# Hash attention and a PReLU MLP in fp32 on one core: the division first in VectorE's round, with weight steps behind its reciprocal, and w_out's operand sums in the MLP's first blocks

## The chip, the cores and the metric

One core of a Trainium2 chip. The metric is the device time of one execution in microseconds (us).

## The reference

```python
# B, H, S, D = 4, 8, 768, 64; proj is 64 x 6; w_in 512 x 2048, w_out 2048 x 512
q_bits, k_bits = (q @ proj > 0), (k @ proj > 0)          # six sign bits per row
mask = bucket(q_bits)[..., :, None] == bucket(k_bits)[..., None, :]
scores = where(mask, q @ k.T / sqrt(D), -1e9)
attn = softmax(scores) @ v
x = attn.transpose(0, 2, 1, 3).reshape(3072, 512)
h = x @ w_in
out = (max(h, 0) + alpha * min(h, 0)) @ w_out
```

All in fp32. Both products of the MLP are made by a seven-product scheme on 2 x 2 blocks (7 products of half size instead of 8), so weights and activations need sums of their blocks as operands.

## The kernel before

Attention runs in 32 rounds, two for each pair of heads. TensorE makes scores of round u+1, then `av` and the row sums `sm` of round u. VectorE adds up probabilities (accp, accd), divides (st, rc, rr, dn, x), and beside that prepares the MLP's weights: each of 32 pieces (16 of w_in, 16 of w_out) is split in two parts in six steps, and four operand sums per group of pieces are made. The finished groups are stored to DRAM (w_in_s, w_out_s) and loaded again in the MLP (`wi` for each first-stage block, `wl` for each second-stage product).

```python
def divide(u, between=lambda: None):
    ...                                                  # cut: tiles
    do(DVE.transpose(a, sums[u]))                        # st
    do(DVE.tensor_scalar(r, a..., S * EPS, None, op0=ALU.add))      # rc
    do(DVE.reciprocal(rr, r...))                         # rr
    for q0 in (0, D):                                    # four small copies on GpSimd
        q1 = q0 + 32
        do(POOL.tensor_copy(rr[q0 : q0 + 32, 1], rr[q1 : q1 + 32, 1]))
        do(POOL.tensor_copy(rr[q1 : q1 + 32, 0], rr[q0 : q0 + 32, 0]))
    between()                                            # here: one or two operand sums
    do(DVE.transpose(d, rr...))                          # dn
    do(DVE.scalar_tensor_tensor(x, av[u], vsum[pi], d, ...))        # x, frees av's bank

for u in range(UNITS):                                   # cut to the parts concerned
    scores(u, 1)
    if u < last:
        scores(u + 1, 0)
    if u:
        divide(u - 1, lambda: weight_sums(1 if u < HW else 2))
    add_last(u)                                          # accd
    add_total(u)
    if u < last:
        add_first(u + 1)                                 # accp; its second half by an accumulating DMA
    ...                                                  # cut: hash bits, q and k turns
    if u < last:
        weight_parts(u + 1)                              # four of the six steps
    attend(u)                                            # av
    totals(u)                                            # sm
    if u < last:
        weight_sum(u + 1)                                # the last two steps
        weight_group(u + 1)                              # queues four sums and the store
    ...
    load_weight(u + 4)
    ...                                                  # at odd u: loads of v, q, k of later pairs

for j, (b, what, n) in enumerate(blocks):                # MLP, cut
    ...
    if what == "1":
        load_w(b * NI + n + 2)                           # wi, double-buffered
        if n >= NI - 2:
            load_w2(b, n - NI + 2)                       # wl
```

In the traces, f_0 to f_7 are the eight blocks of the MLP's first stage and z_1 to z_7 the products of its second; pt are the probabilities, qn, kn and vn the loaded pieces of q, k and v, and vd is a small TensorE step of a range check that needs the largest values (top) from VectorE.

`do` keeps an instruction at its place in its engine's program; transfers issued without it are placed by a scheduler that may move them ahead. Nearly all transfers go through the one queue of SyncE (SPq in the traces; 127.18 of 141.64 MB).

Of the kernel before, what the change touches and what calls it, by code (L numbers as in the profile page):

```python
# [8 lines left out]
F32 = mybir.dt.float32  # L9
# [3 lines left out]
ALU = mybir.AluOpType  # L13
# [393 lines left out]
def fast_path(  # L407
# [60 lines left out]
    NI = NF // 2  # L468
    NM = 7
    w_in_s = dram.tile([NI, P, NM, 2, P], F32, name="w_in_s")  # L470
    w_out_s = dram.tile([NM, P, NI, DM // 2], F32, name="w_out_s")
    x_s = dram.tile([B, NP, P, S], F32, name="x_s")
    NW = NK * NF // 2
    wmax = const.tile([P, NW], F32, name="wmax")
# [68 lines left out]
    def piece(i):  # L543
# [8 lines left out]
        o = n + NI * m  # L552
        return moe_w_out[o * P : (o + 1) * P]

    def load_weight(i):
        if i < NW:
            raw[i] = pool.tile([P, 512], moe_w_in.dtype, name=f"raw{i}", tag="raw", bufs=3)
            nc.sync.dma_start(raw[i], piece(i))

# [5 lines left out]


    def weight_abs(i):
        lo, hi = halves(i)
        wx[i] = pool.tile([P, 512], F32, name=f"wx{i}", tag="wx")
        do(ACT.activation(wx[i], hi.bitcast(F32), AF.Abs))  # L570

    def weight_parts(i):
        lo, hi = halves(i)
        x = wx[i]
        wr[i] = r = pool.tile([P, 512], F32, name=f"wr{i}", tag="wr", bufs=1)
        do(DVE.tensor_scalar(x, x, HI_MIN, None, op0=ALU.max, op1=ALU.max, accum_out=wmax[:, i : i + 1]))  # L576
        do(DVE.tensor_scalar(
            x.bitcast(U32), x.bitcast(U32), 3, 0xC0000000, op0=ALU.logical_shift_left, op1=ALU.bitwise_xor,
        ))
        do(DVE.tensor_scalar(r.bitcast(U32), x.bitcast(U32), 0x7F800000, None, op0=ALU.bitwise_and))  # L580
        do(DVE.scalar_tensor_tensor(r, lo, 2.0 ** -52, r, op0=ALU.mult, op1=ALU.mult))

    def weight_sum(i):


        lo, hi = halves(i)
        x, r = wx[i], wr[i]
        if i < HW:
            n, m = divmod(i, 4)
            if m == 0:  # L590
                wst[n] = pool.tile([P, NM, 4, P], F32, name=f"wsi{n}", tag="wsi")
            slot = (0, 5, 1, 2)[m]
            dst = wst[n][:, slot].rearrange("p i f -> p (i f)")
        else:
            n, m = divmod(i - HW, 2)
            if m == 0:
                wst[HW + n] = pool.tile([P, NM, DM // 2], F32, name=f"wso{n}", tag="wso")
            w = wst[HW + n]
            dst = w[:, 0:6:5] if m == 0 else w[:, 1:3]
        turned = i < HW and m == 3  # L600
        do(DVE.scalar_tensor_tensor(
            r, x, -1.0 if turned else 1.0, r, op0=ALU.mult, op1=ALU.subtract if turned else ALU.add,
        ))
        if i >= HW:
            hi, r = (t.rearrange("p (a f) -> p a f", a=2) for t in (hi, r))
        do(DVE.scalar_tensor_tensor(
            dst.bitcast(U32), hi, 0x80000000, r.bitcast(U32), op0=ALU.bitwise_and, op1=ALU.bitwise_xor,
        ))
# [2 lines left out]

    def weight_group(i):

        if i < HW and i % 4 == 3:
            n = i // 4
            w = wst[n]
        elif i >= HW and i % 2 == 1:
            n = (i - HW) // 2
            w = wst[HW + n]
        else:  # L620
            return
        s1 = ALU.subtract if i < HW else ALU.add
        sums4 = ((3, 5, s1, 2), (5, 0, ALU.subtract, 5), (4, 3, ALU.subtract, 0), (6, 1, ALU.subtract, 4))

        def one(to, a, op, c):
            do(DVE.tensor_tensor(w[:, to], w[:, a], w[:, c], op=op))

        def store():
            if i < HW:
                c, kk = divmod(n, 2)  # L630
                for ii in range(4):
                    nc.sync.dma_start(w_in_s[4 * c + ii][:, :, kk], w[:, :, ii])
            else:
                nc.sync.dma_start(w_out_s[:, :, n].rearrange("m p d -> p m d"), w)

        for x in sums4:
            sums_due.append((one, x))
        sums_due.append((store, ()))

    def weight_sums(count):  # L640
# [266 lines left out]
    def load_w2(b, n):  # L907

        if n < 7:
            t = late[0].tile([P, NI, 2 * H2], F32, name=f"wl{b}_{n}", tag="wl")  # L910
            nc.sync.dma_start(t, w_out_s[SIDES[ORDER[n]][0]])
            for m, kh, dh in ((0, 0, 0), (1, 1, 0), (2, 1, 1), (21, 0, 1)):
                w2[b, n, m] = t.rearrange("p n (f i) -> p n i f", i=2)[:, kh * HK : (kh + 1) * HK, dh]

    def sides_g(b, n):
        t = g_m[b, SIDES[ORDER[n]][1]]
# [138 lines left out]
    weight_abs(0)  # L1055
    weight_parts(0)
    weight_sum(0)
    load_weight(3)
    for name in "qk":
        turn(1, name)  # L1060
    weight_abs(1)
    for u in range(UNITS):
        pi, g = divmod(u, NCH)
        scores(u, 1)
        if u < last:
            scores(u + 1, 0)
        if u:
            divide(u - 1, lambda: weight_sums(1 if u < HW else 2))
        add_last(u)
        add_total(u)  # L1070
        if u < last:
            add_first(u + 1)
        else:
            now = ff1(0, 0)
            now.step(1)
            now.step(5)
        if g == 0 and pi + 1 < NPAIR:
            hash_bits(pi + 1)
        if g == 1 and pi + 2 < NPAIR:
            turn(pi + 2, "q")  # L1080
            turn(pi + 2, "k")
        if u < last:
            weight_parts(u + 1)
        else:
            weight_sums(4)
        attend(u)
        totals(u)
        if u < last:
            weight_sum(u + 1)
            weight_group(u + 1)  # L1090
        else:
            divide(u)
        if g == 1 and pi + 2 < NPAIR:
            load(pi + 2, "v")
        load_weight(u + 4)
        if u == HW + 2:
            load_w(0)
            load_w(1)
            load_x(0)
        if HW + 4 <= u < HW + 8:  # L1100
            sum_x(0, u - HW - 4, DVE)
        if u + 2 < NW:
            weight_abs(u + 2)
        if u == 1:
            setup_alpha()
        if g == 1:
            for name in "qk":
                magnitude(pi, name)
                if pi + 3 < NPAIR:
                    load(pi + 3, name)  # L1110
# [2 lines left out]
    late = []  # L1113
    attn.close()
    late.append(ctx.enter_context(tc.tile_pool(name="late", bufs=2)))
    blocks = [(b, what, n) for b in range(B) for what, count in (("1", NI), ("2", 7)) for n in range(count)]


    for j, (b, what, n) in enumerate(blocks):
# [24 lines left out]
            sum_g2(b, n2, 5)  # L1144
        if j == 4:
            verdict()
        if what == "1":
            load_w(b * NI + n + 2)
            if n >= NI - 2:
                load_w2(b, n - NI + 2)  # L1150
        else:
            load_w2(b, n + 2)
            if b + 1 < B:
                if n == 0:
                    load_x(b + 1)
                if n == 6:
                    for m in range(4):
                        sum_x(b + 1, m, DVE)
# [41 lines left out]
```

## Time and profile before

| | before |
|---|---|
| time, median (lowest to highest) of 4 runs, in the rounds of the changed kernel | 918.46 us (917.09 to 919.78) |
| span of the profiled run | 916.6 us |
| start of the last `sm` (end of attention) | 363.73 us |
| start of the MLP's second stage (first z_1a) | 433.47 us, so 69.74 us after the last sm |
| from z_1a to the end | 483.1 us |
| TensorE waits for VectorE's x in attention | 14.2 us, 18 times |

The last `sm` and the first z_1a cut the span in three: attention, the MLP's first stage, the rest. The profile's lines of attention stand in the prediction. The prediction also reads the time from issue to landing of the wi loads in the MLP's first stage (the view of the tile wi, window 345 to 432 us).

```profile
DMA to landing us min/median/max: 4.3/4.6/6.5
```

Its longest, 6.5 us, was the load that flew just behind two 1 MB loads.

### The profile page before, as it was taken

What the parts mean: (1) busy time and instruction counts of PE and PEld (TensorE: products, weight loads), DVE (VectorE), ACT (ScalarE), POOL (GpSimd) and SP (SyncE); (2) the same over time, 40 slices, a digit from 0 to 9 for tenths busy, and PEclk for the clock granted to TensorE, in tenths of its full rate; (3) what the DMA queues carried; (4) which work ended last, traced back from release to release, by engine and by line L of the source; (5) the groups of instructions that cost most, each with busy time, mean ns of one, the idle gap of its engine ahead of it and who ended that gap; (6) DMA issues with size and microseconds to landing.
All of it is one profiled execution on the core that took longest, in us unless ns stands there. A gap on an engine that the chain in (4) does not pass through costs nothing.

```text
span 916.6 us, 15648 instructions
## 1 busy us (share of the span) xinstructions
PE 888.8 (97%) x5885; PEld 591.8 (65%) x5885; DVE 758.0 (83%) x1353; ACT 409.9 (45%) x735; POOL 70.2 (8%) x178
## 2 busy tenths in 40 slices
PE   8999999999999999999999999999999999999996
PEld 4444444444444444556999556998556998556996
DVE  4888888899999998677989667989777989768985
ACT  7888887788877874222111222111222112222111
POOL 1122121221111121000000000000000000000000
PEclk9999999999999999999999999999999999999998
DMA  9677979799877754534433534333535343521242
GB/s 236 147 182 189 240 196 283 183 219 248 215 187 190 205 133 121 192 112 143 143 115 110 160 121 148 134 109 115 159 118 160 122 124 102 180 95 40 93 152 59
DMA packets 132677, 141.64 MB, mean 155 GB/s; under 512 B 78048, under 2 KB 120816, under 8 KB 129008
## 3 DMA queue, kind: packets, MB, share of 16 engines
q1 hardware_dynamic: 121872, 127.18, 45.3%
q0 software_dynamic: 8704, 12.58, 8.5%
q8 instruction: 48, 0.79, 0.4%
q10 hardware_dynamic: 2016, 0.79, 0.3%
q14 instruction: 37, 0.30, 0.1%
HBM read 100.67 MB, written 27.26 MB: 140 GB/s over the span
## 4 chain that ended last, share of the span: by engine, by line
PE 58%; DMA 1%; DVE 1%; POOL 0%; ACT 0%; issue 0%; ACTq 0%; DVEq 0%; POOLq 0%
PE z_4a L838 2%; PE f_2a L838 2%; PE z_3a L838 2%; PE z_6a L838 2%; PE z_2a L838 2%; PE z_1a L838 2%; PE z_5a L838 2%; PE f_5a L838 2%; PE f_7a L838 2%; PE f_6a L838 2%; PE f_4a L838 2%; PE f_3a L838 2%; PE f_0a L838 2%; PE z_7a L838 2%; PE f_1a L838 2%; PE z_2c L838 1%
## 5 line engine op out<-in xcount | busy, mean ns | idle before, releaser
L723 ACT ACTIVATE pt<-sc 128x768 f32<-128x768 f32 x192 | 152.6, 813 | 63.9 <-PE sc L718 61.9
L718 PE MATMUL sc<-qT,kT 64*128 64x384 f32 x768 | 155.3, 483 | 0.0
L751 PE MATMUL av<-pt,vn 128*32 128x384 f32 (+1 forms) x1536 | 130.6, 488 | 14.4 <-DVE x L792 14.2
L751 PEld LDWEIGHTS av<-pt,vn 128*32 128x32 f32 x1536 | 46.8, 110 | 91.0 <-issue 62.8
L718 PEld LDWEIGHTS sc<-qT,kT 64*128 64x128 f32 x768 | 68.3, 188 | 34.8 <-issue 34.6
L888 DVE TENSOR_TENSOR g<-g,g 128x384 f32<-128x384 f32 x128 | 68.3, 554 | 2.2
L718 PE MATMUL sc<-qb,kb 64*128 64x384 bf16 x384 | 63.5, 324 | 2.8 <-ACT kb L706 1.0
L936 DVE TENSOR_TENSOR gs<-g,gs 128x768 f32<-128x768 f32 x56 | 53.3, 952 | 1.0
L928 DVE TENSOR_TENSOR ws<-wl 128x512 f32<-128x512 f32 x56 | 38.5, 687 | 18.8 <-DMA wl<-w_out_s 18.7
L936 DVE TENSOR_TENSOR gs<-g 128x768 f32<-128x768 f32 x56 | 53.2, 951 | 0.0
L733 POOL DMA_DIRECT2D accp<-pt x32 | 38.5, 1204 | 191.2 <-issue 75.2
L884 DVE SCALAR_TENSOR_TENSOR g<-h,alpha 128x384 f32<-128x384 f32 x32 | 19.7, 617 | 33.4 <-ACT h L877 33.4
L718 PEld LDWEIGHTS <-kb 64*128 64x128 bf16 x384 | 19.5, 94 | 34.4 <-issue 12.3
L695 ACT ACTIVATE qb<-hs,hb 32x384 bf16<-32x384 f32 x62 | 35.5, 573 | 1.1
L789 DVE STREAM_TRANSPOSE dn<-rr 128x384 f32<-128x384 f32 x32 | 18.5, 578 | 21.1 <-POOL rr L787 21.1
L741 DVE TENSOR_TENSOR accd<-accd,accp 128x768 f32<-128x768 f32 x32 | 30.7, 958 | 5.2 <-DMA accp<-pt 4.2
L738 DVE TENSOR_TENSOR accd<-accd,pt 128x768 f32<-128x768 f32 x32 | 30.7, 959 | 3.3
L732 DVE TENSOR_TENSOR accp<-pt,pt 128x768 f32<-128x768 f32 x32 | 30.4, 951 | 2.6 <-ACT pt L723 2.6
L737 DVE TENSOR_TENSOR accd<-pt,pt 128x768 f32<-128x768 f32 x32 | 30.4, 949 | 0.0
L948 DVE TENSOR_TENSOR m<-m,m 128x768 f32<-128x768 f32 (+1 forms) x40 | 28.3, 709 | 1.0 <-ACT m L954 0.3
L706 ACT ACTIVATE kb<-hs,hb 64x384 bf16<-64x384 f32 (+1 forms) x47 | 27.1, 577 | 0.6
L576 DVE TENSOR_SCALAR_CACHE_REDUCE wx<-wx 128x512 f32<-128x512 f32 x32 | 21.7, 679 | 2.9 <-ACT wx L570 2.9
(334 smaller groups left out, 1782.6 us busy)
## 6 DMA issues: line engine op xcount, KB each, us to landing
wi<-w_in_s SPq DMA_DIRECT2D x32, 896.0 KB, 4.6
wl<-w_out_s SPq DMA_DIRECT2D x28, 1024.0 KB, 4.9
accp<-pt POOLq DMA_DIRECT2D x32, 384.0 KB, 4.4
raw<-in_moe_w_in_dram SPq DMA_DIRECT2D x16, 512.0 KB, 4.6
raw<-in_moe_w_out_dram SPq DMA_DIRECT2D x16, 512.0 KB, 3.7
w_in_s<-wsi SPq DMA_DIRECT2D x16, 448.0 KB, 5.9
w_out_s<-wso SPq DMA_DIRECT2D x8, 896.0 KB, 4.5
vn<-in_v_dram SPq DMA_DIRECT2D x16, 384.0 KB, 5.2
```

Of the source, the lines that this page charges most:

```text
L695: do(ACT.activation(bits["q", pi][D * s : D * s + 32, cols], ps["q"][c : c + 32, half, :CW], AF.Sign, bias=hb[c : c + 32],))
L718: do(PE.matmul(sc[:, s, :CW], what["k", pi][r, ks], what["q", pi][r, qs], start=first, stop=not first,))
L723: do(ACT.activation(pt[:, :, :CW], sc[:, :, :CW], AF.Exp, scale=SCALE / DOWN))
L732: do(DVE.tensor_tensor(accp[u], p(u, 0), p(u, 1), op=ALU.add))
L733: nc.gpsimd.dma_start(accp[u], p(u, 2), accum_op=ALU.add)
L738: do(DVE.tensor_tensor(accd[u], accd[u], p(u, 5), op=ALU.add))
L741: do(DVE.tensor_tensor(accd[u], accd[u], accp[u], op=ALU.add))
L751: do(PE.matmul(av[u][D * s + t : D * s + t + 32, :w], nat["v", pi][:, s, kc * D + t : kc * D + t + 32], prob[u, kc][:, s, :w], start=(kc = ...
L838: do(PE.matmul(self.ps[bank], self.left(left, k), self.right(right, k), start=start and k == 0, stop=k == self.nk - 1, skip_group_check=no ...
L888: do(DVE.tensor_tensor(new_g(b, to)[:, i], g_m[b, x][:, i], g_m[b, y][:, i], op=ALU.subtract))
L928: do(DVE.tensor_tensor(t, w2[b, n, x], w2[b, n, y], op=op))
L936: do(DVE.tensor_tensor(t, g2[b, n, x], g2[b, n, y], op=ALU.subtract))
```

## The change

The intent: take VectorE off attention's critical path. The division comes first in VectorE's round, and the last two weight steps stand behind the reciprocal, in the wait for GpSimd's copies (21.1 us in 32 rounds before); at most one operand sum follows at the round's end. The 32 sums of w_out leave attention: the raw parts are stored to w_out_r, and in the MLP's first six blocks, where VectorE has idle time (2.75 us of a block of 9.03 us before), they are loaded again, summed, and stored to w_out_s. The order of the pieces is mixed (w_in over the first 26 of 32 turns).

```diff
+    TURNS = NW * 13 // 16
+    order, left = [], [list(range(HW)), list(range(HW, NW))]
+    for i in range(NW):
+        ahead = (i + 1) * HW // TURNS > HW - len(left[0])
+        order.append(left[0 if left[0] and ahead or not left[1] else 1].pop(0))
 ... (each weight function begins with i = order[i])
     def weight_group(i):
+        if i >= HW:                      # w_out: store the parts, no sums
+            n, m = divmod(i - HW, 2)
+            if m == 1:
+                nc.sync.dma_start(w_out_r[:, :, n]..., wst[HW + n])
+            return
 ...
+    def load_out(n):
+        if n < NI:
+            w_o[n] = late[0].tile([P, 8, DM // 2], F32, name=f"wo{n}", tag="wl")
+            nc.sync.dma_start(w_o[n][:, :4], w_out_r[:, :, n]...)
+    def sum_out(n):
+        w = w_o[n]
+        for to, x, op, y in (four sums):
+            do(DVE.tensor_tensor(w[:, to], w[:, x], w[:, y], op=op))
+        nc.sync.dma_start(w_out_s[:, :, n]..., w[:, 4:])
+        load_out(n + 2)
 ...
     for u in range(UNITS):
         if u:
-            divide(u - 1, lambda: weight_sums(1 if u < HW else 2))
+            divide(u - 1, weight_rest)   # weight_sum(u), weight_group(u)
+        load_weight(u + 3)
 ...
             weight_parts(u + 1)
-        else:
-            weight_sums(4)
+        weight_sums(1)
         attend(u)
         totals(u)
-        if u < last:
-            weight_sum(u + 1)
-            weight_group(u + 1)
-        else:
+        if u == last:
             divide(u)
 ...
-        load_weight(u + 4)
 ... (MLP)
+        for n_out in [(0,), (1, 2), (3,), (4, 5), (6,), (7,)][j] if j < 6 else ():
+            sum_out(n_out)
         if what == "1":
             load_w(b * NI + n + 2)
```

More of the change, by code (lines that the diff above doesn't have):

```diff
@@ L470, in fast_path @@
     w_in_s = dram.tile([NI, P, NM, 2, P], F32, name="w_in_s")
-    w_out_s = dram.tile([NM, P, NI, DM // 2], F32, name="w_out_s")
+    w_out_r = dram.tile([4, P, NI, DM // 2], F32, name="w_out_r")
+    w_out_s = dram.tile([4, P, NI, DM // 2], F32, name="w_out_s")
     x_s = dram.tile([B, NP, P, S], F32, name="x_s")
@@ L553, in piece @@
         return moe_w_out[o * P : (o + 1) * P]
+    TURNS = NW * 13 // 16
[3 more added lines that the diff above has]
+        order.append(left[0 if left[0] and ahead or not left[1] else 1].pop(0))
     def load_weight(i):
         if i < NW:
+            i = order[i]
             raw[i] = pool.tile([P, 512], moe_w_in.dtype, name=f"raw{i}", tag="raw", bufs=3)
@@ L567, in weight_abs @@
     def weight_abs(i):
+        i = order[i]
         lo, hi = halves(i)
@@ L572, in weight_parts @@
     def weight_parts(i):
+        i = order[i]
         lo, hi = halves(i)
@@ L583, in weight_sum @@
     def weight_sum(i):
+        i = order[i]
         lo, hi = halves(i)
@@ L596, in weight_sum @@
             if m == 0:
-                wst[HW + n] = pool.tile([P, NM, DM // 2], F32, name=f"wso{n}", tag="wso")
+                wst[HW + n] = pool.tile([P, 4, DM // 2], F32, name=f"wso{n}", tag="wso")
             w = wst[HW + n]
-            dst = w[:, 0:6:5] if m == 0 else w[:, 1:3]
+            dst = w[:, 0:4:3] if m == 0 else w[:, 1:3]
         turned = i < HW and m == 3
@@ L612, in weight_group @@
     def weight_group(i):
-        if i < HW and i % 4 == 3:
-            n = i // 4
-            w = wst[n]
-        elif i >= HW and i % 2 == 1:
-            n = (i - HW) // 2
-            w = wst[HW + n]
-        else:
+        i = order[i]
+        if i >= HW:
+            n, m = divmod(i - HW, 2)
+            if m == 1:
+                nc.sync.dma_start(w_out_r[:, :, n].rearrange("m p d -> p m d"), wst[HW + n])
             return
-        s1 = ALU.subtract if i < HW else ALU.add
-        sums4 = ((3, 5, s1, 2), (5, 0, ALU.subtract, 5), (4, 3, ALU.subtract, 0), (6, 1, ALU.subtract, 4))
+        n, m = divmod(i, 4)
+        if m < 3:
+            return
+        w = wst[n]
         def one(to, a, op, c):
@@ L628, in store @@
         def store():
-            if i < HW:
-                c, kk = divmod(n, 2)
-                for ii in range(4):
-                    nc.sync.dma_start(w_in_s[4 * c + ii][:, :, kk], w[:, :, ii])
-            else:
-                nc.sync.dma_start(w_out_s[:, :, n].rearrange("m p d -> p m d"), w)
-        for x in sums4:
-            sums_due.append((one, x))
+            c, kk = divmod(n, 2)
+            for ii in range(4):
+                nc.sync.dma_start(w_in_s[4 * c + ii][:, :, kk], w[:, :, ii])
+        for x in ((3, 5, 2), (5, 0, 5), (4, 3, 0), (6, 1, 4)):
+            sums_due.append((one, (x[0], x[1], ALU.subtract, x[2])))
         sums_due.append((store, ()))
@@ L910, in load_w2 @@
             t = late[0].tile([P, NI, 2 * H2], F32, name=f"wl{b}_{n}", tag="wl")
-            nc.sync.dma_start(t, w_out_s[SIDES[ORDER[n]][0]])
+            m = SIDES[ORDER[n]][0]
+            nc.sync.dma_start(t, w_out_r[m] if m < 3 else w_out_s[m - 3])
             for m, kh, dh in ((0, 0, 0), (1, 1, 0), (2, 1, 1), (21, 0, 1)):
                 w2[b, n, m] = t.rearrange("p n (f i) -> p n i f", i=2)[:, kh * HK : (kh + 1) * HK, dh]
+    w_o = {}
+    def load_out(n):
+        if n < NI:
+            w_o[n] = late[0].tile([P, 8, DM // 2], F32, name=f"wo{n}", tag="wl")
+            nc.sync.dma_start(w_o[n][:, :4], w_out_r[:, :, n].rearrange("m p d -> p m d"))
+    def sum_out(n):
+        w = w_o[n]
+        for to, x, op, y in ((4, 3, ALU.add, 2), (6, 0, ALU.subtract, 3), (5, 4, ALU.subtract, 0), (7, 1, ALU.subtract, 5)):
+            do(DVE.tensor_tensor(w[:, to], w[:, x], w[:, y], op=op))
+        nc.sync.dma_start(w_out_s[:, :, n].rearrange("m p d -> p m d"), w[:, 4:])
+        load_out(n + 2)
     def sides_g(b, n):
@@ L1057, in fast_path @@
     weight_sum(0)
-    load_weight(3)
     for name in "qk":
@@ L1063, in fast_path, with weight_rest @@
         pi, g = divmod(u, NCH)
+        def weight_rest():
+            weight_sum(u)
+            weight_group(u)
         scores(u, 1)
@@ L1083, in fast_path @@
             weight_parts(u + 1)
-        else:
-            weight_sums(4)
+        weight_sums(1)
         attend(u)
         totals(u)
-        if u < last:
-            weight_sum(u + 1)
-            weight_group(u + 1)
-        else:
+        if u == last:
             divide(u)
@@ L1115, in fast_path @@
     late.append(ctx.enter_context(tc.tile_pool(name="late", bufs=2)))
+    load_out(0)
+    load_out(1)
     blocks = [(b, what, n) for b in range(B) for what, count in (("1", NI), ("2", 7)) for n in range(count)]
```

## The prediction

> **What bounds the kernel now.** I read the page first, then the waits of TensorE and VectorE, then their timelines round by round.
>
> ```profile
> PE 888.8 (97%) x5885; PEld 591.8 (65%) x5885; DVE 758.0 (83%) x1353; ACT 409.9 (45%) x735; POOL 70.2 (8%) x178
> PE   8999999999999999999999999999999999999996
> DVE  4888888899999998677989667989777989768985
> ```
>
> TensorE is busy 97% of the span, so at most 27.8 us can be won without removing matmuls. The MLP (from about 364 us, slice 16 on) is all TensorE: nothing to win. What is left is in attention, 32 rounds up to 364 us, where VectorE stands at 8 and 9 tenths. The waits of attention (10 to 368 us):
>
> ```profile
> DVE dn L789 <- POOL rr L787: 21.1, 32, 1.0
> DVE accd L741 <- DMA accp<-pt: 4.2, 2, 2.3
> DVE st L781 <- PE sm L763: 0.5, 1, 0.5
> PE av L751 <- DVE x L792: 14.2, 18, 1.3
> ```
>
> VectorE waits for TensorE's sums (st <- sm) once in 32 rounds, while TensorE waits 18 times for VectorE's x, which frees the accumulator bank. So **VectorE's chain sets the pace of attention**, and TensorE is not far behind it. One VectorE round, from st to st (cut; start, duration):
>
> ```profile
> 81.98 0.38 DVE L781 STREAM_TRANSPOSE st<-sm 128x192 f32<-128x192 f32 x1
> 82.59 0.23 DVE L783 RECIPROCAL rr<-rc 128x12 f32<-128x12 f32 x1
> 82.74 0.63 DVE L626 TENSOR_TENSOR wsi<-wsi 128x512 f32<-128x512 f32 x1
> 84.11 0.58 DVE L789 STREAM_TRANSPOSE dn<-rr 128x384 f32<-128x384 f32 x1 [0.74 <-POOL rr L787]
> 84.72 0.62 DVE L792 SCALAR_TENSOR_TENSOR x<-av,vs,dn 128x384 f32<-128x384 f32 x1
> ...
> 90.70 0.69 DVE L581 SCALAR_TENSOR_TENSOR wr<-raw,wr 128x512 f32<-128x512 uint32 x1
> 91.42 0.69 DVE L601 SCALAR_TENSOR_TENSOR wr<-wx,wr 128x512 f32<-128x512 f32 x1
> 92.15 0.69 DVE L606 SCALAR_TENSOR_TENSOR wsi<-raw,wr 128x512 uint32<-128x512 uint32 x1
> 92.76 0.15 DVE L775 TENSOR_SCALAR vs<-av 128x1 f32<-128x1 f32 x1
> 92.83 0.37 DVE L781 STREAM_TRANSPOSE st<-sm 128x192 f32<-128x192 f32 x1
> ```
>
> A round with a w_in sum lasts 10.78 us (10.85 with vs, every second one); one with two w_out sums 10.63 (303.24 to 313.86); the four with an x sum (L811) about 11.5. TensorE's own round is read where it never waited, early on:
>
> ```profile
> 57.98 0.51 PE L763 MATMUL sm<-accd,ones 128*32 128x192 f32 x8
> 64.17 4.09 PE L751 MATMUL av<-pt,vn 128*32 128x385 f32 x48
> 68.08 0.51 PE L763 MATMUL sm<-accd,ones 128*32 128x192 f32 x8
> 74.93 4.08 PE L751 MATMUL av<-pt,vn 128*32 128x384 f32 x48
> 78.82 0.51 PE L763 MATMUL sm<-accd,ones 128*32 128x192 f32 x8
> ```
>
> 10.10 us in a round with hash bits, 10.74 in one with the q and k turns: 10.42 on average, against VectorE's 10.6 to 10.8.
>
> [...] GpSimd's four small copies (rr) take 0.18 us alone, but beside two w_in sums:
>
> ```profile
> 193.34 0.44 POOL L786 COPY rr<-rr 32x6 f32<-32x6 f32 x1 [2.88 <-DVE rr L783]
> 193.82 0.56 POOL L787 COPY rr<-rr 32x6 f32<-32x6 f32 x1
> 194.43 0.18 POOL L786 COPY rr<-rr 32x6 f32<-32x6 f32 x1
> ```
>
> The first copy ends with the first sum, the second with the second sum: one copy gets through per VectorE instruction. [...] the trace has 692 (L601) and 958 (L741). So the moved steps cost the same wherever they stand. [...] the SP queue stood 34.9 us in four waits for f_4a. It matters for the rivals.
>
> **The change part by part.**
> 1. *weight_sum (L601, L606) moves from the round's end to behind the reciprocal.* At the end it goes with 0.73 + 0.61 us of spacing, and L581 before it gets 0.11 shorter in spacing (0.72 to 0.61, as it is no longer followed by an instruction that needs it): -1.45. Behind the reciprocal stood one w_in sum, with rr to dn 1.52 us. Two steps there, by the one-copy-per-instruction pattern: 0.15 to the first, 0.72 to the second, 0.69 for it, then two more copies at 0.22 and some 0.1 of signalling: 2.1 us (estimate). So a round without any sum is 10.78 - 1.45 - 1.52 + 2.10 = **9.91 us**. The GpSimd wait is not filled: about 0.6 of it stays, since the steps block the copies.
> 2. *w_in sums at the round's end, one at most.* 16 of them, each about 0.55 of spacing (204.34 to 204.89). Stepping the diff's order by hand, they fall in rounds 6-9, 12-15, 19-22 and 25-28. Such a round is 10.46. On average 9.91 + 0.28 + 0.04 for vs = 10.23, under TensorE's 10.42.
> 3. *32 w_out sums (11.2 us busy) leave attention* for MLP blocks 0 to 5, 4 or 8 in a block, 1.4 or 2.8 us. A block lasts 9.03 us there and VectorE idles 2.75 of it (0.86 + 0.58 + 1.31), so they lie beside TensorE's work. New transfers: 8 loads and 8 stores of 512 KB; the earlier w_out stores get smaller by as much.
> 4. *Mixed pieces* even out the sums; alone worth nothing.
>
> **The sum.** From sm of round 4 (68.08) to sm of round 31 (363.73) is 295.65 us. TensorE alone needs 12 x 10.75 + 12 x 10.10 for rounds 5 to 28, 2 x 9.35 (rounds 29 and 30: 10.68 less 1.33 and 10.64 less 1.28 of waits) and 9.7 (10.68 less 0.97): 278.6. So **17.0 us can be won there**, and 0.8 at round 2, where scores waited for VectorE's alpha copy. What stays: VectorE may lag about 1.6 us in hash and 2.3 us in turn rounds (sm to av is 6.2 or 6.85; st to the end of x about 4 us, and 0.57 ahead of it). Rounds 20 to 22 carry an x sum (0.87) and a w_in sum, 11.33 against 10.10 and 10.75; the lag passes the limits by 0.3 + 0.5 + 0.8 = 1.6 us. In rounds 29 and 30 TensorE has no hash and no turns, and VectorE's 9.9 against 9.35 with little slack costs 1.5. So 17.8 - 3.1 = 14.7 won in attention. For the MLP's added traffic I take 0.5 off (judgement). 919.2 - 14.2 = **905 us**.
>
> **The rivals.**
> - *The copies are held through both steps, or the steps are held by the copies.* Then rr to dn is 2.5 or more, the round 10.3 and with sums 10.65, and VectorE still leads. Gain about 7: 912. Against it: one copy got through per sum in every round seen.
> - *The MLP gives it back.* The load of wi for block n+2 can go only when block n's last matmul has read the buffer: 372.0 to 378.5, 6.45 us for a transfer of 4.6 (median); the one at 372.20 took 6.5 beside two 1 MB loads and TensorE waited. Now each block also has 512 KB stores and loads on the same queue, and a reload must wait for its store. If such a wait stands ahead of a wi load, each block loses 1 to 5 us: 908 to 920. For it: the tight 1.8 us. Against: the 512 KB pieces are half of what flew at 372, and the two 1 MB loads come later.
> - *The accumulating DMA (accp) becomes the wait.* It lands in 4.4 us (median) but once in 10.6, and cost VectorE 2.3 us at 152. With VectorE ahead of TensorE such a miss is mostly absorbed; some 1 to 2 us if not.
> - *Attention runs wholly at TensorE's pace:* 901.
>
> **Range and chances.** The gain's ceiling is 17.0 + 0.8 + 0.3 (the wi wait) = 18.1 us, below 2% (18.4), so faster by over 2% is nearly out: 0.04. Everything seen to go wrong costs less than the gain, so slower by over 2%: 0.01. The range runs from nearly no waits left, 901.5, to the first rival or a mild second one, 911.
>
> **What would show it.** Right: rr to dn near 2.1 us with two stretched copies; VectorE waiting for sm (st <- sm) in most rounds up to 19; rounds alternating 10.10 and 10.75 on TensorE; PE's waits for x down from 14.2 to about 3 us, in rounds 21 to 24 and 29 to 31; the last sm near 349; MLP blocks still 9.03. Wrong: rr to dn of 2.5 and no wait for sm (first rival), or blocks of the first MLP stage longer than 9.03 with waits for wi or wl (second).

## The result, and the profile after

| | before | after |
|---|---|---|
| median (lowest to highest), 4 runs each | 918.46 us (917.09 to 919.78) | 911.77 us (910.37 to 913.69) |
| ratio | | 0.9929, 95% interval 0.9902 to 0.9955 |
| span of the profiled run | 916.6 us | 910.8 us |
| start of the last sm | 363.73 us | 352.12 us |
| last sm to first z_1a | 69.74 us | 75.32 us |
| z_1a to the end | 483.1 us | 483.4 us |
| all transfers | 141.64 MB | 146.88 MB |

A ratio is the mean time of one kernel's fast runs over that of the kernel before in the same rounds, so not quite the ratio of the medians. The kernel is 0.7% faster: "same" at the 2% mark, as was thought most likely, but 911.77 is 0.8 us beyond the range's end of 911. Attention won 11.6 us and the MLP's first stage gave 5.6 back; of the 14.2 us forecast, 3.1 were missing in attention and 5.3 in the MLP, which leaves the 5.8 us by which the profiled spans differ.

VectorE's line on the page, in 40 slices, and TensorE's:

```profile
PE   8999999999999999999999999999999999999996
DVE  4988898988998997887989768989768989768985
```

The waits of VectorE and TensorE (in total, times, longest):

```profile
DVE dn L799 <- POOL rr L797: 17.5, 32, 1.0
DVE st L791 <- PE sm L773: 8.5, 6, 2.6
PE tp_k L669 <- DMA kn<-in_k_dram: 3.2, 2, 1.7
PE av L761 <- DVE x L802: 2.6, 5, 0.8
PE f_4a L848 <- DMA wi<-w_in_s: 1.4, 1, 1.4
PE f_6a L848 <- DMA wi<-w_in_s: 1.3, 1, 1.3
PE f_7a L848 <- DMA wi<-w_in_s: 1.3, 1, 1.3
PE vd L1041 <- DVE top L1034: 0.9, 1, 0.9
```

TensorE's waits for x fell from 14.2 us to 2.6, and VectorE now waits for TensorE (st <- sm), though in five of rounds 0 to 19 only (two of them are rounds 11 and 17, where TensorE itself stood for kn), not in most, as the prediction's signs have it. Two new kinds stand beside them: twice TensorE stood before turning k because the k load had not landed (kn), and three times in the MLP because wi had not.

VectorE's round behind the reciprocal, and GpSimd's copies beside it, cut:

```profile
58.12 0.23 DVE L793 RECIPROCAL rr<-rc 128x12 f32<-128x12 f32 x1
58.26 0.63 DVE L613 SCALAR_TENSOR_TENSOR wr<-wx,wr 128x512 f32<-128x512 f32 x1
58.92 0.69 DVE L618 SCALAR_TENSOR_TENSOR wsi<-raw,wr 128x512 uint32<-128x512 uint32 x1
60.15 0.58 DVE L799 STREAM_TRANSPOSE dn<-rr 128x384 f32<-128x384 f32 x1 [0.53 <-POOL rr L797]
58.48 0.44 POOL L796 COPY rr<-rr 32x6 f32<-32x6 f32 x1 [2.28 <-DVE rr L793]
58.97 0.69 POOL L797 COPY rr<-rr 32x6 f32<-32x6 f32 x1
59.70 0.19 POOL L796 COPY rr<-rr 32x6 f32<-32x6 f32 x1
```

From rr to dn it is 2.03 us. The first copy ends with the first step, the second with the second, as the prediction said.

Now the two new waits. SyncE's queue around the first kn wait (TensorE stood until 137.37 us):

```profile
120.38 4.24 SPq L643 DMA_DIRECT2D w_in_s<-wsi  x4
124.71 1.37 SPq L489 DMA_DIRECT2D vn<-in_v_dram  x1
128.32 3.54 SPq L500 DMA_DIRECT2D kn<-in_k_dram  x2
```

The four stores of a w_in group wait for its last sum, which VectorE now makes at the end of the round. They stand ahead of this round's loads of v, q and k, so the loads start after 124.71 us. In the pair before, the k load was issued at 100.21 us, so two rounds of some 10.4 us later it would have gone near 121. In the kernel before, the same sum stood early in the next round, so the store came behind the loads (loads from 125.80 us, stores at 130.67).

The queue and TensorE around f_4a in the MLP:

```profile
376.72 1.74 SPq L932 DMA_DIRECT2D wo<-w_out_r  x2
378.65 0.36 SPq L827 DMA_DIRECT2D wi<-w_in_s  x1
386.49 1.56 PE L848 MATMUL f_4a<-x,wi 128*128 128x384 f32 x4 [1.42 <-DMA wi<-w_in_s]
```

The wi load left on time, 0.2 us after the last matmul (378.46) that read its buffer; nothing blocked its issue. But 1 MB of wo had been issued in the two microseconds ahead of it, and it landed after 7.8 us. The loads for f_6a and f_7a had 1 MB ahead, wo and wl, and landed after 7.8 and 7.7 us. The load for f_5a (389.37 us) had only 512 KB ahead, yet it too took 7.0 us; it made nobody wait, as vd, just before f_5a, had waited 0.9 us itself. Bytes ahead are thus not the whole of it in this kernel; the order of the queue is tested below. For the whole stage (same view and window as before):

```profile
DMA to landing us min/median/max: 4.8/7.0/7.8
```

TensorE's four stops (three for wi, one for vd) are 4.9 us of waits. Measured from start to start of its matmuls, with the slower first ones behind the stops (four in 1.56 us behind each wait for wi, in 1.45 elsewhere), they are 5.9 us, nearly all of what this stretch is longer than the 69.36 us of m_ord3 below.

### The profile page after: what moved, and what is told of

It reads as the page before. It is cut to its first block, busy times and chain, and to the rows that moved or that the text cites.

```text
span 910.8 us, 15639 instructions
## 1 busy us (share of the span) xinstructions
PE 888.5 (98%) x5885; PEld 590.7 (65%) x5885; DVE 756.1 (83%) x1353; ACT 410.5 (45%) x735; POOL 88.5 (10%) x178
## 2 busy tenths in 40 slices
DMA packets 138053, 146.88 MB, mean 161 GB/s; under 512 B 78304, under 2 KB 126192, under 8 KB 134384
## 4 chain that ended last, share of the span: by engine, by line
PE 55%; DMA 5%; DVE 2%; issue 0%; POOL 0%; ACT 0%; ACTq 0%; DVEq 0%; POOLq 0%
PE z_4a L848 2%; PE f_7a L848 2%; PE z_3a L848 2%; PE z_6a L848 2%; PE z_5a L848 2%; PE z_2a L848 2%; PE z_1a L848 2%; PE f_0a L848 2%; PE f_1a L848 2%; PE f_6a L848 2%; PE z_7a L848 2%; PE f_5a L848 2%; PE f_4a L848 2%; PE f_2a L848 2%; PE f_3a L848 2%; DMA wi<-w_in_s 2%
## 5 line engine op out<-in xcount | busy, mean ns | idle before, releaser
L954 DVE TENSOR_TENSOR ws<-wl 128x512 f32<-128x512 f32 x56 | 38.5, 687 | 18.9 <-DMA wl<-w_out_s 15.9
L797 POOL COPY rr<-rr 32x6 f32<-32x6 f32 x64 | 27.6, 432 | 2.6
```

What stands on the lines that cost most here:

```text
L954: do(DVE.tensor_tensor(t, w2[b, n, x], w2[b, n, y], op=op))
```

## The experiments

My first theory had two parts: stores ahead of loads cost attention 3.2 us, and wi loads that land late behind other transfers cost the MLP some 5 us. The rivals: mixing, or more transfers as such; SyncE blocking; and VectorE's lag in the MLP. Eighteen runs were made, one of them the changed kernel again, five rounds each and always with the kernel before on the same chip. All gave the correct result.

| kernel | median us | ratio to before | last sm, us | last sm to z_1a, us |
|---|---|---|---|---|
| before | 917.4 to 918.5 | 1 | 363.73 | 69.74 |
| changed | 911.77 | 0.9929 | 352.12 | 75.32 |
| changed, again (after_r) | 912.28 | 0.9951 | 351.99 | 75.76 |
| b_mlp | 921.60 | 1.0041 | 361.52 | 75.62 |
| a_attn | 912.24 | 0.9938 | 358.60 | 69.35 |
| a_attn_nm | 915.86 | 0.9976 | 364.50 | 69.35 |
| a_store | 909.95 | 0.9912 | 350.51 | 75.15 |
| a_nomix | 907.97 | 0.9888 | 349.73 | 74.39 |
| a_behind | 925.25 | 1.0074 | 367.06 | 74.96 |
| a_behind_st | 921.31 | 1.0035 | 361.47 | 76.25 |
| m_split | 923.69 | 1.0064 | 352.92 | 82.96 |
| best | 923.23 | 1.0058 | 349.68 | 87.13 |
| m_ord | 931.10 | 1.0143 | 354.00 | 78.77 |
| m_ord2 | 931.74 | 1.0151 | 352.55 | 78.88 |
| m_ord3 | 917.69 | 0.9999 | 354.24 | 69.36 |
| m_ord4 | 911.31 | 0.9931 | 353.02 | 69.68 |
| m_ord5 | 908.12 | 0.9902 | 354.08 | 69.35 |
| best2 | 912.20 | 0.9938 | 348.12 | 70.26 |
| best3 | 904.39 | 0.9856 | 348.10 | 69.36 |
| best4 | 901.90 | 0.9839 | 348.23 | 69.35 |

### One part of the change alone

**b_mlp**: the kernel before with the MLP part only.

```diff
 # on the kernel before: w_out_r, load_out, sum_out as in the change, pieces unmixed
+        for n_out in [(0,), (1, 2), (3,), (4, 5), (6,), (7,)][j] if j < 6 else ():
+            sum_out(n_out)
```

> The kernel before with the change's MLP part alone: w_out sums leave attention for the MLP's first blocks, nothing else moves. Theory (the MLP part costs 5 us in the MLP, and the 32 sums it takes from attention were nearly free there, as they stood in the wait for GpSimd's copies): last sm 363.7 -> about 361 to 363, last sm to first z_1a 69.7 -> 75, time 918.5 + 3 to 5 = 921 to 923. Rival of the prediction (11.2 us of VectorE work leave VectorE's critical chain, the MLP absorbs it): time 910 to 914.

Measured 921.6 us: attention won 2.2 us and the MLP lost 5.9. The 11.2 us of sums that left were nearly free where they stood, in the wait for GpSimd's copies: VectorE's round fell from 10.63 us with two of them to 10.51 without. The MLP part by itself is a loss.

**a_attn**: the changed kernel with the w_out sums left in attention.

```diff
-        weight_sums(1)
+        weight_sums(4 if u == last else 2)
 # and: no w_out_r, load_out, sum_out
```

> The changed kernel with the w_out sums kept in attention (at most two sums a round at its end, four in the last), so the MLP is that of the kernel before. Theory (the reorder in attention is what wins; the MLP part costs more than it wins): last sm at about 353 to 356 (rounds with two sums behind 9.91 come to 10.6, as in the kernel before), last sm to first z_1a back at about 70, time about 908 to 910, no worse than the changed kernel's 911.8. Rival (moving the w_out sums out was needed for the gain): last sm at 359 or later, time 914 or more.

Measured 912.24 us, last sm at 358.60: later than I expected (353 to 356), before the rival's 359. The MLP is back at 69.35 us. So, with the reorder, moving the sums to the MLP is worth 6.5 us in attention (358.60 - 352.12) and costs 6.0 there (75.32 - 69.35): as built, it won next to nothing. In this kernel the kn waits are larger (4.8 us in three places), and TensorE waits for x 7.3 us.

**a_attn_nm**: the same, with the pieces unmixed.

```diff
-    TURNS = NW * 13 // 16
+    TURNS = HW
```

> The reorder in attention with the w_out sums kept in attention (912.2 us) and the pieces unmixed besides, so that the w_in stores meet no loads. It asks whether the sums had to go to the MLP at all. Theory (kn waits, 4.8 us in three places, are half slack of VectorE, as in the run with stores behind loads): kn waits under 1.7 us, waits for x up from 7.3 to 9, last sm at about 356, z_1a 69.4 behind, time 909 to 910, so 5 to 6 us above the kernel with both mends. Rival (without kn waits attention runs at TensorE's pace): last sm at 353 or earlier, time 906 or less.

Both expectations failed: 915.86 us. The kn waits did go. But unmixed, the w_in sums come in pairs in every second pair of rounds, those rounds measured 11.2 us on TensorE, and rounds 21 to 24, which also have an x sum, 11.5 to 11.6. Once VectorE also waited 4.8 us for an accumulating DMA (accp), and TensorE 3.3 us for VectorE: the prediction's third rival, which cost most here. So with two sums a round mixing may help, but it is not shown: this one late transfer is most of the 3.6 us between the two runs.

### Attention: the stores ahead of the loads

**a_store**: the stores are issued one round later, behind the loads.

```diff
     def weight_sums(count):
-        while sums_due and (count or sums_due[0][0].__name__ == "store"):
+        while sums_due and count and sums_due[0][0].__name__ == "one":
 ...
         load_weight(u + 3)
+        while sums_due and sums_due[0][0].__name__ == "store":
+            sums_due.pop(0)[0]()
 # and do(...) around these stores and the loads of q, k, v, so that they keep this order
```

> The changed kernel with only the queue order mended: the w_in_s stores are issued in the next round, behind the loads of q, k and v. Theory (a store that waits for VectorE's last w_in sum stands ahead of the k load, twice): TensorE's two waits for kn (3.2 us) go, the last sm comes at about 349 instead of 352.1, and the time falls from 911.8 to about 908.7. Rival (VectorE's pace takes back what TensorE no longer waits): kn waits go, but waits for x or scores grow by as much, the last sm stays near 352 and the time near 911.5. The MLP stays at 75.3 us from the last sm to the first z_1a in both.

The kn waits went, but the last sm moved from 352.12 only to 350.51, of which 0.7 was an earlier start of the run. Waits for x rose from 2.6 to 5.2 us, as the rival had it in numbers; in rounds 21 to 24 TensorE waited 2.8 us for x instead of 1.1. But the reason is not VectorE's pace. Up to round 17 VectorE kept level with TensorE without the stops (its st 0.58 us behind the start of sm, about as close as it ever comes). Then it waited 2.65 us for the accumulating DMA accp, issued at 200.82 us and landed after 10.2:

```profile
211.14 0.96 DVE L751 TENSOR_TENSOR accd<-accd,accp 128x768 f32<-128x768 f32 x1 [2.65 <-DMA accp<-pt]
```

In the changed kernel the same accp landed after 9.4 us and nobody waited, because TensorE, and VectorE behind it, had just stood for kn. So the stops had hidden the prediction's third rival.

**a_nomix**: the changed kernel with the pieces unmixed (same one-line diff as a_attn_nm). Its stores fall in rounds without loads.

> The changed kernel with the pieces unmixed (w_in first, then w_out), so the four w_in_s stores fall in rounds 6, 10, 14 and 18, which have no loads of q, k and v, and a w_in sum stands in each of rounds 3 to 18. Theory (queue order costs 3.2 us, mixing itself little): kn waits are gone; rounds 20 to 24 lose their w_in sums beside the x sums, so waits for x shrink by about 1; rounds 3 to 18 run at 10.46 against TensorE's 10.42, at most 1 us more. Last sm about 349, time about 908.5. Rival (the mixing is what lets VectorE keep up): waits for x grow in rounds 5 to 18 and the last sm comes later than 352, time 912 to 914.

It came as the theory said: kn waits gone, waits for x still 2.6 us, last sm at 349.73, time 907.97. In rounds 3 to 18 a sum in each round cost TensorE at most 0.9 us of wait for x, and 0.9 for accd; both came just after VectorE had waited 3.3 us for a late accp (150.54 us). With the w_out sums in the MLP, mixing is not needed: it costs some 4 us (911.8 or 912.3 against 908.0), 2.4 of them in attention, where it puts stores ahead of loads.

### Attention: what stands behind the reciprocal

**a_behind**: the two weight steps behind x.

```diff
-        between()
         do(DVE.transpose(d, rr...))
         do(DVE.scalar_tensor_tensor(x, av[u]..., d, ...))
+        between()
```

> The changed kernel with the two weight steps behind x instead of behind the reciprocal. Theory of the prediction (the copies get through one per VectorE instruction, so the two steps hide in a wait that lasts about 1.2 anyway, and cost 2.0 of which 0.8 beyond the bare wait): rr to dn falls from 2.03 to about 1.2, x comes 0.85 earlier, but the round gets 0.5 to 0.6 longer, 10.4 without a sum and 11.0 with one: VectorE bounds rounds with sums again, waits for x come back (8 to 12 us), time 916 to 920. Rival (the copies are blocked through both steps, so standing behind the reciprocal hides nothing): rr to dn about 1.2 and a round no longer than 9.9, time 911 to 912.

Measured 925.25 us, more than the 916 to 920 expected. Two rounds with the stores lasted 15.9 and 15.6 us on TensorE (12.5 and 12.6 in the changed kernel): all of VectorE's later work, the last w_in sum and its store too, came later. So this run mixes two causes, and was repeated without one.

**a_behind_st**: the same with the stores behind the loads (the edit of a_store).

> The weight steps behind x, with the w_in_s stores issued behind the loads. Against a_store (910.0 us, the same but for the steps behind the reciprocal) it tells what hiding the steps in the wait for the copies is worth. Theory (prediction: a VectorE round gets some 0.5 us longer, which costs where VectorE leads: rounds 20 to 31 and rounds after sums): kn waits gone, waits for x about 10 us, last sm at 357 to 359, time 916 to 919. Rival (the loss of the run with the steps behind x was all in the kn waits, VectorE has the slack): last sm at 352 or earlier, time 912 or less.

Measured 921.31 us and the last sm at 361.47, both 2.3 us or more beyond what I expected. Against a_store, the same kernel with the steps behind the reciprocal, the last sm comes 11.0 us later, of which 1.3 is a later start of the run; from the first sm to the last it is 9.7 us. One division:

```profile
209.94 0.23 DVE L793 RECIPROCAL rr<-rc 128x12 f32<-128x12 f32 x1
211.20 0.58 DVE L798 STREAM_TRANSPOSE dn<-rr 128x384 f32<-128x384 f32 x1 [1.03 <-POOL rr L797]
```

rr to dn is 1.26 us with nothing between, 2.03 with two steps that take 1.33 us elsewhere: hiding them saves 0.56 us a round. A round without a sum (st at 47.65 and 58.05) lasts 10.40 us, against 9.91 in the changed kernel (st at 36.89 and 46.80). So half a microsecond on VectorE's round, where TensorE's needs 10.42 and sums come on top, is worth about 10 us.

### The MLP: what lies ahead of a load

**m_split**: the w_out pieces in buffers of their own, one piece in each block.

```diff
-            w_o[n] = late[0].tile([P, 8, DM // 2], F32, name=f"wo{n}", tag="wl")
+            for h in range(2):           # two halves, buffers of ws3 and ws4
+                t = late[0].tile([P, HK, H2], F32, name=f"wo{n}_{h}", tag=f"ws{3 + h}", bufs=2)
 ...                                     # sums into two tiles of tag m
-        for n_out in [(0,), (1, 2), (3,), (4, 5), (6,), (7,)][j] if j < 6 else ():
+        for n_out in [(0,), (1,), (2,), (3,), (4,), (5,), (6, 7)][j] if j < 7 else ():
```

> The changed kernel with the w_out pieces of the MLP in buffers of their own (256 KB halves), and one piece in each of the first blocks instead of one, two, one, two: a wi load finds at most about 512 KB issued ahead of it, and the wl loads don't wait for the pieces' buffers. Theory (the wi loads land late because up to 1 MB of wo or wl is issued 1 to 2 us ahead [...]): the waits of f_4a, f_6a and f_7a (4.0 us) shrink to under 0.5 and vd's 0.9 goes; last sm to first z_1a 75.3 -> about 70.5, time about 907. Rival 1 (VectorE is late in the MLP because of the moved sums, whatever the transfers): blocks stay long, z_1a 74 to 75, time 911. Rival 2 (the added megabytes cost, however spread): the waits move to other blocks and their sum stays at 3 to 4 us.

A miss by nearly 17 us, 923.69. The queue and TensorE show why:

```profile
359.38 0.47 SPq L922 DMA_DIRECT2D wl<-w_out_r  x1
363.36 1.83 SPq L935 DMA_DIRECT2D wo<-w_out_r  x2
365.24 0.53 SPq L827 DMA_DIRECT2D wi<-w_in_s  x1
365.82 0.50 SPq L922 DMA_DIRECT2D wl<-w_out_r  x1
372.50 2.93 PE L848 MATMUL f_2a<-x,wi 128*128 128x384 f32 x4 [4.68 <-DMA wi<-w_in_s]
```

The wl loads had shared buffers with the pieces, and that had held them back. With free buffers the scheduler moved both 1 MB loads to the very start, and wi was issued late (at 365.24, where it goes at 360.59 in the changed kernel) and among them. f_2a waited 4.7 us, f_4a 2.8, f_7a 2.6. The run refutes the mend, not the theory: I had changed what lies ahead of wi in the wrong direction.

**best**: m_split, a_store's edit and the largest-value reductions two blocks earlier (`if j == 2`).

> Both mends together (stores behind loads; pieces in own buffers, one a block) and the largest-value reductions moved two blocks earlier. Theory (the two losses are independent, on TensorE's path): -3.2 in attention, -4.0 -0.9 in the MLP: 911.8 - 8.1 = about 903.7, over 1.5% faster than before. Rival (they share slack, or each mend only moves a wait): 907 or more.

Measured 923.23 us, for the same reason (f_2a waited 5.5 us). It shows nothing beyond m_split.

**m_ord**: the changed kernel's buffers, and a fixed order on the queue: wi, then the piece's store, then the next piece's load.

```diff
-            nc.sync.dma_start(w_m[n], w_in_s[n % NI])
+            do(nc.sync.dma_start(w_m[n], w_in_s[n % NI]))       # also for wl, wo, w_out_s
 ...
             load_w(b * NI + n + 2)
+            for n_out in outs:           # one piece a block, the last block two
+                store_out(n_out)
+                load_out(n_out + 2)
```

> The changed kernel with the MLP's transfers kept in a fixed order on their queue: in each block the wi load first, then the store of the finished w_out piece, then the load of the next piece (which has to wait for that store, as it reuses the buffer); one piece a block (the last block two), the wl loads at their place behind. Bytes, sums and buffers are the same as in the changed kernel. After the split-buffer run, whose two 1 MB wl loads slipped ahead of the first wi load and made f_2a wait 4.7 us, the theory is that what is issued ahead of a wi load within some 3 us sets how late it lands. Theory: only the 512 KB load of a piece is still 3 us ahead of a wi load; f_4a, f_6a and f_7a wait under 1 us together, last sm to first z_1a 75.3 -> about 71.5, time about 908. Rival (bytes per block decide, order doesn't): waits of 3 to 4 us stay and the time stays at 911 to 912. Rival (fixed order makes the queue itself block, as the piece's load waits for its store ahead of the next wi load): new waits for wi, 913 or more.

**m_ord2**: the same order with m_split's buffers, piece load ahead of piece store.

> As the run before, but with the pieces in buffers of their own as in the split-buffer run, so that the next piece's load doesn't wait for the store: in each block wi, piece load, piece store are issued together, wi first, and the wl loads stay behind at their place. It differs from the split-buffer run (923.7 us) by queue order alone. Theory (order ahead of wi decides): wi lands in about 4.6 to 5 us as in the kernel before, no wait for wi over 0.3, last sm to first z_1a about 70 to 71, time about 907. Rival (the split buffers or the bytes themselves cost the 12 us of the split-buffer run): time stays at 918 or more.

Both took 931 us, more than 20 above what the theory said. Yet the waits for wi did what the theory said: 1.3 us in all in m_ord, none listed in m_ord2, where wi landed in a median of 5.0 us (window 345 to 432 us) and then the second stage stood:

```profile
DMA to landing us min/median/max: 4.8/5.0/6.7
431.43 2.90 PE L848 MATMUL z_1a<-g,wl 128*128 128x192 f32 x8 [9.27 <-DMA wl<-w_out_r]
```

The fixed order had put the wl loads behind the last stores, in three batches (13.1 us in m_ord2). Without the first of these waits the stretch would be 78.88 - 9.27 = 69.6 us, as in the kernel before. For wi, m_ord2 against m_split is the plain test: bytes, sums and buffers are the same, only the order on the queue differs, and 10.1 us of waits for wi go to none.

**m_ord3**: m_ord2 with the first batch's wl loads right behind the wi loads of blocks 5 and 6; later batches left to the scheduler.

```diff
             load_w(b * NI + n + 2)
+            if b == 0 and n in (NI - 3, NI - 2):
+                load_w2(0, n - NI + 3)
```

> The run with pieces in own buffers and wi, piece load, piece store in this order (931.7 us), changed in one thing: the wl loads of the first batch go right behind the wi loads of blocks 5 and 6 instead of behind the last stores, and later batches' wl loads are left to the scheduler as in the changed kernel. In the 931.7 us run all waits for wi had gone but z_1a waited 13.1 us for wl, in three batches; without the first of these waits the stretch from the last sm to z_1a was 69.6 us. Theory (what stands or flies ahead of a load decides, for wi and wl alike): no wait for wi over 0.5 us, z_1a's wait for wl under 1, last sm to z_1a 70 to 71, time 906 to 907.5. Rival (the bytes themselves must cost somewhere, the wait only moves on): wi or wl waits of 3 us or more and 910 or more.

The stretch is 69.36 us: with the same bytes and sums as the changed kernel, and with m_split's buffers, the order brought the MLP's first stage back. But the time, 917.69 us, was 10 too high, mostly because of one wait behind it:

```profile
432.78 2.93 PE L848 MATMUL z_1b<-g,wl 128*128 128x192 f32 x8 [6.43 <-DVE f_7p L890]
```

VectorE stood for the store of piece 6, whose output buffers piece 7 was to reuse: a wait of my own edit. These eight matmuls took 2.93 us here and 1.46 elsewhere, and the granted clock was 0.50 from 432 to 436 us. Matmuls were slow behind another long wait too: in m_split, four matmuls of a first-stage block took 2.93 us behind a wait of 4.68 us (f_2a), 1.56 behind one of 2.79 us (f_4a), and 1.45 without a wait. So this wait cost some 1.6 us beyond itself (estimate: 3.2 us of work, 432.78 to 436, at the granted clock of 0.50), and the totals of runs with waits as long as these hold more than the waits. The rest of the 10 us is attention, whose last sm came 2.1 us later than in the changed kernel.

**best2**: m_ord3 with unmixed pieces.

> The run m_ord3 with the weight pieces unmixed (w_in first) as in a_nomix, which removed the kn waits and won 3.8 us on the changed kernel, 2.4 of it in attention. Theory (the two are independent): last sm at 349.7, MLP stretch 70 to 71, time about 903 to 904.5, 1.5 to 1.7% under the kernel before. Rival (a_nomix's gain in the MLP, 1 us, was the same gain as m_ord3's, or attention gives back): 905 or more.

The same wait (6.3 us) and 912.2 us, but attention as hoped: last sm at 348.12, no wait for x listed.

**m_ord4** and **best3**: the two again, with the sums of odd pieces in buffers of their own.

```diff
-        t  = late[0].tile([P, 2, CW], F32, name=f"wq{n}", tag="m", bufs=3)      # and wr
+        tags = (("m", 3), ("m", 3)) if n % 2 == 0 else (("m1", 1), ("m5", 1))
```

> m_ord3 with one thing changed: odd pieces put their sums into two buffers of their own (those of m1 and m5, unused in this stage), so that piece 7's sums don't wait for piece 6's store. Theory (MLP loss is queue order, the 6.4 us wait of z_1b was my buffer's): no wait over 1 us in the MLP, last sm to z_1a about 70, z_1a to the end 483 to 484.5 as in the two kernels, time 906 to 908 (5 under the changed kernel). Rival (the added bytes cost 4 to 5 us wherever): new waits of 4 us or more and 911 or more.

> best2 (unmixed pieces and ordered MLP) with the same buffers. In best2 the last sm came at 348.1 and z_1a 70.3 later, then z_1b waited 6.3 us. Theory: that wait goes, time 912.2 - 8 = 902.5 to 905, over 1.4% under the kernel before. Rival as above: 909 or more.

best3 met its expectation: 904.39. m_ord4 did not (911.31 for 906 to 908), though its profiled run had a span of 907.7. VectorE made two pieces in block 6 and waited 1.3 us for store buffers, and TensorE waited 2.1 us at the start of the second stage.

**after_r**, **m_ord5** and **best4**: the changed kernel again, and the two with the double block early.

```diff
-        outs = [(0,), (1,), (2,), (3,), (4,), (5,), (6, 7)][j] if j < 7 else ()
+        outs = [(0,), (1, 2), (3,), (4,), (5,), (6,), (7,)][j] if j < 7 else ()
```

> The changed kernel again, unaltered, as the reference on the same chip for the next two runs. Both theories: about 911.8 us, ratio to the kernel before 0.993; waits of f_4a, f_6a and f_7a about 4 us together, of kn 3.2.

> m_ord4 with the pieces two in block 1 and one in each other (blocks 0 to 6), so that the last block sums one piece and finds its buffers free. Theory (the MLP's loss was queue order and then VectorE's late pieces): waits of z_1a, z_1c and z_2c fall from 2.1 to under 0.8, last sm to z_1a 69.5 to 70, z_1a to the end 483.5, and the timed ratio to after_r of the same chip is about 0.994, that is 5 to 6 us less. Rival (the profile flatters: the added traffic costs elsewhere in unprofiled runs): within 1.5 us of after_r.

> best3 (904.4 us) with the same split of pieces. Theory: 1 to 1.5 us less, 903 us, 1.6% under the kernel before. Rival: no change, 904.4.

On one chip: changed 912.28 (ratio 0.9951), m_ord5 908.12 (0.9902), best4 901.90 (0.9839). m_ord5's MLP is as expected (69.35 us, no wait of over 0.4 us, 482.2 us from z_1a to the end), but its gain is 4.2 us and not 5 to 6, as its last sm came 2.1 us later: TensorE waited 4.5 us for x instead of 2.6. The traces of m_ord to m_ord5 show where this comes from. In the changed kernel the first two wi loads leave at 198.10 us; in these runs the scheduler put them at about 212, 3 us ahead of an accp transfer, which then landed after 9.0 to 10.3 us instead of 6.5. In m_ord3:

```profile
212.25 0.98 SPq L827 DMA_DIRECT2D wi<-w_in_s  x2
215.11 1.20 POOL L743 DMA_DIRECT2D accp<-pt  x1 [5.59 <-issue]
225.48 0.96 DVE L751 TENSOR_TENSOR accd<-accd,accp 128x768 f32<-128x768 f32 x1 [2.66 <-DMA accp<-pt]
```

VectorE waited 2.7 us for it in m_ord3, 2.4 in m_ord5 and 1.4 in m_ord4, and TensorE's waits for x are longer by 2.2, 1.9 and 1.2 us. This is read from the traces; no run moves these two loads alone. best4 was 1.1 us better than I expected.

**A better version.** best4 beats both kernels: 1.6% under the kernel before, 1.1% under the changed one. Its edits are the unmixed pieces and, in the MLP, the ordered queue with the w_out pieces in buffers of their own. It still loses some 2.7 us in rounds 20 and 21 (10.57 and 12.99 us on TensorE), where an accp landed after 9.6 us.

## Why the prediction was right or wrong

**VectorE's chain sets attention's pace: right.** Waits for x fell from 14.2 to 2.6 us when the chain got shorter, and half a microsecond more on it cost about 10 us (a_behind_st against a_store).

**rr to dn at 2.1 us, one copy per VectorE instruction: right.** Measured 2.03, with 0.53 of wait left. A round without a sum lasted 9.91 us, as forecast, and one with a w_in sum 10.44 to 10.52 (forecast 10.46). That is level with TensorE's 10.42, so the sign "VectorE waits for sm in most rounds up to 19" did not show (five times). The first of the two moved steps took 0.63 us behind the reciprocal and 0.69 at the round's end, so "cost the same wherever they stand" is right to 0.06 us. **TensorE's rounds of 10.10 and 10.75: right**, read again as 10.10 and 10.74.

**The lag terms: right, with luck in the first.** For the lag of rounds 20 to 22 I took 1.6 us, the trace has 1.1 (rounds 23 and 24); for rounds 29 to 31, 1.5 and 1.5 (0.84 + 0.49 + 0.19). Without the kn stops a late accp makes the first one 2.8 (a_store), so it held because another loss hid this one. The 0.8 at the alpha copy was won.

**Attention wins 14.7: wrong by 3.1 us.** The last sm came at 352.12, not near 349. The sum has no term for the two kn waits (3.2 us). My step 2 worked out in which rounds the sums fall, and did not ask what waits for the last sum of a group: a store, in a queue where loads stand behind it. a_nomix moves the stores away and has the last sm at 349.73. That the wait is not the whole story shows in a_store: only part of it comes back, as TensorE's stops had hidden a late accp. So the third rival was real as well, at about the 2 us that it names.

**"For the MLP's added traffic I take 0.5 off": this is the term that failed most.** The MLP's loss measured 5.8 us (552.9 us from the last sm to the end before, 558.7 after). With attention's miss alone, the sum would have come to 908. The second rival had the right place, but its mechanism, a wait ahead of wi on the queue, was not what happened: wi was issued at once and landed late. The argument against it ("half of what flew at 372", "the two 1 MB loads come later") was wrong on both counts: two 512 KB loads went together in every second block, which makes 1 MB, and the wl loads, held back by the shared buffers, came right ahead of wi at 409 and 419 us. What the runs put in its place: with 1 MB ahead wi lands after 7.7 to 7.8 us and TensorE waits 1.3 to 1.4 us; with wi first it lands in a median of 4.8 to 5.1 us, and the stretch is back at 69.4 us (m_ord3, m_ord5), with the same bytes. An estimate that fits these loads: in 415 to 425 us of m_ord3 the transfers moved 342 GB/s, so 1 MB takes 3.1 us, and 7.8 - 4.6 = 3.2. It does not fit the load for f_5a: 512 KB ahead, by the same rate 1.5 us, and it took 2.4 longer.

**w_out's sums "lie beside TensorE's work": right for the sums, wrong for their transfers.** vd's wait of 0.9 us is VectorE's only direct cost there, as VectorE stood for wo loads.

**"Attention runs wholly at TensorE's pace: 901":** this rival is nearly best4 at 901.9, where no wait for x is left. The gain was there; the change as built gave it back on the queue.

**What stays open.** Why the wi load for f_5a took 7.0 us with half the bytes ahead. And whether the late accp transfers go away when nothing large is issued just ahead of them: the traces suggest it, no run tests it.

## What to carry to other kernels

When work moves from one engine's critical path to a stage with idle time, cost its transfers as well as its instructions: look up, for the load with the least slack, how many bytes will be issued just ahead of it, and issue that load first (here wi landed after 7.7 to 7.8 us with 1 MB ahead, in a median of 4.8 to 5.1 us when it went first). Look at every queue for this: accp, which GpSimd issues, was late behind loads of SyncE (9.0 to 10.3 us instead of 6.5). A store that waits for a late result must not stand ahead of loads that could go (3.2 us of waits for kn). And when a buffer is given up, look what it had held back: freed transfers move forward, into the way of others (4.7 us of wait for f_2a in m_split).
